# A two-branch token mixer on one core: an eighths fold in the channel transform, and a scan over every second token

## The chip, the cores and the metric

The kernel runs on one core of one Trainium2 chip. The metric is the device time of one execution in microseconds (us), as the median of several runs.

## The reference

The input x has S = 2048 tokens of D = 1024 channels in bf16. Two branches are mixed per token:

```python
g = sigmoid((x * gate_w).sum(-1, keepdims=True))
a = irfft2(rfft2(x) * (w_r + 1j * w_i))           # over tokens and channels
# b: a diagonal state space model
Lam_bar = exp(exp(log_dt) * Lambda)
Bu = einsum("bld,pd->blp", x, B_bar)               # B_bar from B_re, B_im, Lam_bar, Lambda
for t in range(L): h = Lam_bar * h + Bu[:, t]      # complex, 1024 states
b = 2 * einsum("blp,dp->bld", h, C).real + x * Dskip
out = g * a + (1 - g) * b
```

## The kernel before

The kernel is written out by hand for five engines: PE (matmul), DVE (vector), ACT (scalar), POOL and SP (DMA issue). Each step of the computation is a Python generator (`turn`, `fold`, `fd`, `unit_mm`, ...), and a long string `ORDER` holds one letter for each next step of one of them; the order of the letters is the order of the instructions in every engine's queue. The four PSUM buffers are dealt out by the string `SLOTS`. The pieces of the recurrence stand in a list `work`, and each letter `v` issues the next one by the index list `PIECES`. No scheduler changes any of it afterwards. An engine runs its queue in order and waits where an operand or a buffer isn't ready.

The spectral branch begins with the channel transform. `turn` and `turn_out` (PE L919, ACT L929) transpose x into `xQ`. x is treated in 16 row groups j. `fold` on DVE (L943 to L954) makes sums and differences of the two halves of the channels, then of the quarters, into `preT`. For the last four groups of instructions (`MIRROR`, that is eight row groups) PE reverses two blocks of the odd half (`mirror`, L970, into `ps_r`) and `fold_odd` on DVE (L976, L977) adds and subtracts them. `fd` multiplies the result with constant tables on PE, `fd_out` brings it to SBUF as `X1` (L449 on ACT, some on DVE), `s1` starts the token transform. Later stages (`s2`, `times_w`, `is1`, `is2`, `spectral`) go through the frequencies and back.

The state space branch works on eight chunks of 256 tokens. `unit_mm` (L398) makes, for each chunk, four groups of 32 matmuls B x into PSUM (`psu`), and `unit_out` (L408, ACT) copies each to a tile `h` in SBUF. There are three such tiles, so chunk 3's first copy must wait until the products of chunk 0 are done. `recur` makes the recurrence a real scan: it multiplies the states with rotation tables (`cross` L347, `along` L350, `join_re` L353, `join_im` L356), adds the carry of the chunk before (L359), runs the scan over the real and the imaginary part (L363), takes the carry of this chunk (L368, L371) and rotates back (L347, L350, `out_re` L374, `out_im` L378). Chunks 0 and 1 go through this in two halves of four state blocks, the other six whole:

```python
work.extend((lambda: cross(1), lambda: along(0), join_re, join_im))
if c:
    work.append(carry_in)
work.extend((lambda: scan(0, 0, n), lambda: scan(1, 0, n)))
if c + 1 < NCH:
    work.extend((carry_part, carry_sum))
work.extend((lambda: cross(3), lambda: along(2), out_re, out_im))
```

`early_mm` (`c_half`, L713) and, for the last tiles, `own_mm` (`c_part`, L727) multiply h with C for token tiles of 128 tokens, two to a chunk. ACT scales the result (L744), and it is stored or added to the spectral part. The tables of the rotation come from `make_tab`: angles (L279, and on DVE), sine and cosine on ACT (from L1106 on), casts to bf16 (L287, L294, on POOL or ACT by `CAST_ACT`). `radii` (L268) writes the radii that the scan reads on POOL. `turn_vectors` (L1080, L1082) brings the parameters into the layout that all this needs. `load_B` fetches B by transposing DMAs.

Of the kernel before, what the change touches and what calls it, by code (L numbers as in the profile page):

```python
# [25 lines left out]
TC = 256  # L26
NCH = S // TC
# [11 lines left out]
CAST_ACT = (5, 6, 7)  # L39
ANG_ACT = (4, 5, 6, 7)  # L40
CARRY_POOL = ()
# [9 lines left out]
)  # L51
SLOTS = (
    "0123012310231023102310230123012031201312031203101230132031231031201312303312013213021021013010320130",
    "1220123203201320130130120321023120320321021023120312301230231201302303120",
)
MIRROR = (6, 7, 8, 9)
ORDER = (
    "xxxTVUVVVaTfVVrrUGTGG|Tfaaa|UafFffftafftUftxFEfTETUFffU22xSEkSTSTArxAfffUAUFTTEUfffUFbxwxbxbbTUEFbfE",
    "1bT~SSUfuFSFAUUUU2bbtbfAF1AtbbtrFttrbEffE11EbEh11SStbttfttttAg1~HtfufhA~tetFSSFrKHrtu1EAvfAEhtttvttt",
    "SSFtbbvvvAtEttH1Avthtftv1cttwv1tcthccctttvtcch~HFtvftHvvhuHtvfStEettStAHhtAeKrvFctcvvFhEEHKtvwtcSvtS",  # L60
    "hvvKc1vcc1vAAKKvv1c1v1hcvswcsLMvvveHHekMYsssnNHvvhHnsvvvJWWMvs3vsvNvvsssssnvssnvvs4NMvv4Njvhv553vhvv",
    "YvyJJL46H4vv5WWvhh5vvvMM78Jj7HHmn3nHvv8M44m6MnN77WW5jv+Yy5vvv3M845+mNY8nMJJMyvvv+467hvHMh5vN7N34vHmh",
    "4J8m+6n3h8v77HmH+55v4n64JMvNnMYy5vW83n+v7N474vJ568vYmmNJ7dh7NWj+v58v5vyvvd88MhvHHm8+MJm6h+n378vv7Hh8",
    "J+d4Y4YX5vv5NnJH6XXv7ny7mNNm8+hn8hvqivvvvvJvqyHihYivvyiqhivqqiYvNImvni+qJJmHIIiini+HinvdIIH+vvIIIqIN",
    "IiiiNmI+vvIInvvImvyJqii%NJINIJYJYmhvvv+vvvlylzvhHmplpzZZH+mZZZhlZvhPPRR++zyRRRlQDQHzRZZmRHZ+ZRZvoOZD",
    "QvlpDzzPovOvQBvZZlpPYvZZvBZDZRDRRRvzQDoloOBzoQOopZOoPOBlzlZRoDDZZvBZZRpQvzCvYZZvZZBZZPRDoQoo9RQQ9yRR",
    "0RRyCooD099C9Y990DD0D0Y00",
# [6 lines left out]
HALF_PI = float(np.pi / 2)  # L74


def _host_consts():
# [9 lines left out]
    Ge = np.stack([G[0, :H, :, e::2] for e in range(2)])  # L87
    Gf = np.concatenate([G[0, :P, :, 2 * f::4].reshape(P, P) for f in range(2)], axis=1)
    Go = np.stack([G[1, :, :, e::2] for e in range(2)], axis=1)
# [3 lines left out]
    for u in range(4):  # L93
# [25 lines left out]
    angM = 2 * np.pi * (((64 * (f % 32) + 16 * (f // 32) + np.arange(16)[None, :, None]) * np.arange(32)[None, None, :]) % S) / S  # L119
# [11 lines left out]
        G=b16(np.concatenate([Go.reshape(4, P, 4 * K // 4).transpose(1, 0, 2).reshape(P, 4 * K),  # L131
                              Ge.reshape(2, 2, P, H).transpose(2, 0, 1, 3).reshape(P, 4 * H), Gf], axis=1)),
# [10 lines left out]
def kernel(  # L143
# [19 lines left out]
    out2 = out[0]  # L163

    hc = _host_consts()
    cG = nc.inline_tensor(hc["G"], name="c_G").ap()
# [49 lines left out]
    tau_i = tmp.tile([P, TC], I32, name="tau_i")  # L216
    nc.gpsimd.iota(tau_i, pattern=[[1, TC]], base=0, channel_multiplier=0)

# [4 lines left out]
    tab = tabp.tile([P, 4, 8, TC], BF16, name="tab")  # L223
# [6 lines left out]
    fft["G"] = pre.tile([P, 4 * K + 5 * H], BF16, name="G_sb")  # L230
# [19 lines left out]
    def load_G():  # L250
        for a, b in ((4 * K, 4 * K + 5 * H), (0, 2 * K), (2 * K, 4 * K)):
            nc.sync.dma_start(out=fft["G"][:, a:b], in_=cG[:, a:b])
            yield
# [9 lines left out]
    def cast(i):  # L263
        return nc.scalar.copy if i in CAST_ACT else nc.gpsimd.tensor_copy

    def radii():
        for jb in range(8):
            nc.gpsimd.tensor_copy(out=rz[:, jb, :], in_=r_sb[:, jb:jb + 1].to_broadcast([P, TC]))  # L268
            nc.gpsimd.memset(rz[:, jb, 0:1], 0.0)
            yield  # L270

    def make_tab(jp):
        sh = [P, 2, TC]
        js = slice(2 * jp, 2 * jp + 2)
        ang = tmp.tile(sh, FP32, name="ang", tag="ang")
        for j in range(2):
            jb = 2 * jp + j
            if jb in ANG_ACT:
                nc.scalar.activation(out=ang[:, j], in_=tau_f, func=ACT.Copy, scale=thp[:, jb:jb + 1])  # L279
            else:  # L280
                nc.vector.tensor_scalar_mul(out=ang[:, j], in0=tau_f, scalar1=thp[:, jb:jb + 1])
            yield
        sn_f = tmp.tile(sh, FP32, name="sn_f", tag="sn_f")
        cs_f = tmp.tile(sh, FP32, name="cs_f", tag="cs_f")
        yield from sincos(tmp, ang, sh, sn_f, cs_f, "rot")
        yield
        cast(2 * jp)(out=tab[:, 1, js, :], in_=sn_f)  # L287
        yield
        t1 = tmp.tile(sh, FP32, name="t1")
        t2 = tmp.tile(sh, FP32, name="t2")  # L290
        for j in range(2):
            nc.scalar.activation(out=t1[:, j], in_=sn_f[:, j], func=ACT.Copy, scale=ci[:, 2 * jp + j:2 * jp + j + 1])
        yield
        cast(2 * jp + 1)(out=tab[:, 0, js, :], in_=cs_f)  # L294
        yield
        for j in range(2):
            jb = 2 * jp + j
            nc.scalar.activation(out=t2[:, j], in_=cs_f[:, j], func=ACT.Copy, scale=ci[:, jb:jb + 1])
        yield
        for j in range(2):  # L300
            jb = 2 * jp + j
            nc.vector.scalar_tensor_tensor(out=tab[:, 2, jb, :], in0=cs_f[:, j], scalar=cr[:, jb:jb + 1], in1=t1[:, j],
                                           op0=ALU.mult, op1=ALU.subtract)
            yield
        for j in range(2):
            jb = 2 * jp + j
            nc.vector.scalar_tensor_tensor(out=tab[:, 3, jb, :], in0=sn_f[:, j], scalar=cr[:, jb:jb + 1], in1=t2[:, j],
                                           op0=ALU.mult, op1=ALU.add)
            yield

    rz = tabp.tile([P, 8, TC], FP32, name="rz")
    carry = cpool.tile([P, 2, 8], FP32, name="carry")
# [5 lines left out]
    def halloc():  # L318
        pool = hpool[hcount[0] % (NHA + NHB) >= NHA]
        hcount[0] += 1  # L320
        return pool.tile([P, 2, 8, TC], BF16, name="h")
# [7 lines left out]
    def small_ops():  # L329
        return nc.gpsimd if next(smalls_made) in CARRY_POOL else nc.vector  # L330

    smalls_made = itertools.count()

    def recur(c, js, home):
        n = js.stop - js.start
        on_in, on_part, on_sum = (small_ops() for _ in range(3))
        sh = [P, 2, n, TC]
        u = hs[c][:, :, js, :]

        def bc(i):  # L340
            return tab[:, i:i + 1, js, :].to_broadcast(sh)

        tmps = {}

        def cross(i):
            tmps["s"] = home()
# [869 lines left out]
```

## Time and profile before

| | |
|---|---|
| runs | 307.19 us median of 3 (306.89, 307.19, 309.19) |
| the profiled execution's own time | span of 303.6 us from the first to the last instruction, 3.6 us less than the median of the runs |
| granted clock of PE | 0.999 |
| busy PE, DVE, ACT, POOL | 296.4, 289.3, 188.5, 73.3 us |
| DMA | 59.35 MB, 196 GB/s in the mean |
| first product of h with C | at 82.5 us |

Busy times are of one execution, taken by the profiler. The row of a group has the line and the engine, the tiles written and read, the shape, how often it ran, its busy time in all, and the mean of one in ns; what stands behind the last bar is the idle time just before, with the instruction that ended it. A row of the timeline begins with the start and the duration in us.

### The profile page before, as it was taken

Reading aid. Unit: us, or ns where it says so; the run is one execution under the profiler, and the core shown is the slowest. Engines: PE = TensorE matmul, PEld = TensorE weight load, DVE = VectorE, ACT = ScalarE, POOL = GpSimd, SP = SyncE. Lnnn points to the kernel's source line nnn. Section 1 sums busy time; section 2 is a strip of 40 time slices with the busy share of each in tenths; the row PEclk is TensorE's granted clock in tenths of the full one; section 3 lists DMA queues with packets and bytes.
Section 4 is the critical chain, followed back from the end, with each engine's and each line's share of the span. In section 5 each row is a group of like instructions: output and inputs, shape, how many; then the busy total and the mean of one; then the engine's idle time right before and its main releaser. Section 6 shows DMA issues by size and latency. Waiting matters only on the chain. (4 is left out here: it accounts for less than half of the span.)

```text
span 303.6 us, 6402 instructions
## 1 busy us (share of the span) xinstructions
PE 296.4 (98%) x2568; PEld 197.4 (65%) x2592; DVE 289.3 (95%) x340; ACT 188.5 (62%) x255; POOL 73.3 (24%) x99
## 2 busy tenths in 40 slices
PE   8999999999999999999999999999999999999995
PEld 5664677878864685458553866669657986645543
DVE  2999999999999999999999999999899999999995
ACT  4999999896532383667665865529668774343400
POOL 2100420745893001110210220202011253252330
PEclk9999999999999999999999999999999999999999
DMA  6999999989999599895948798687758876978976
GB/s 208 341 201 194 253 193 310 162 142 154 268 214 241 160 259 219 181 250 189 212 96 258 163 223 225 139 294 147 242 174 185 165 88 135 160 132 143 165 153 181
DMA packets 74157, 59.35 MB, mean 196 GB/s; under 512 B 44904, under 2 KB 61680, under 8 KB 74128
## 3 DMA queue, kind: packets, MB, share of 16 engines
q1 hardware_dynamic: 66560, 49.82, 65.8%
q0 software_dynamic: 6912, 8.69, 23.0%
q10 hardware_dynamic: 656, 0.44, 0.5%
q8 instruction: 20, 0.33, 0.4%
q14 instruction: 9, 0.07, 0.1%
HBM read 27.46 MB, written 23.08 MB: 166 GB/s over the span
## 5 line engine op out<-in xcount | busy, mean ns | idle before, releaser
L398 PE MATMUL psu<-xQ,BT 128*128 128x256 bf16 x1024 | 116.5, 273 | 0.2 <-DVE X L449 0.2
L398 PEld LDWEIGHTS <-BT 128*128 128x128 bf16 x1024 | 99.0, 98 | 17.3 <-issue 4.6
L713 PE MATMUL ps_y<-CT,h 128*128 128x512 bf16 x397 | 92.5, 379 | 0.9
L363 DVE TENSOR_TENSOR_SCAN h<-rz,h 128x2048 bf16<-128x2048 f32 (+1 forms) x20 | 70.8, 3561 | 0.0
L713 PEld LDWEIGHTS <-h 128*128 128x128 bf16 x416 | 39.6, 98 | 46.3 <-issue 2.9
L785 POOL DMA_DIRECT2D y_scratch<-su x20 | 17.3, 902 | 135.7 <-ACT su L779 105.4
L408 ACT CAST h<-psu 128x1024 bf16<-128x1024 f32 x32 | 32.3, 1011 | 18.7 <-PE psu L398 13.1
L350 DVE TENSOR_TENSOR h<-h,tab 128x4096 bf16<-128x4096 bf16 (+1 forms) x20 | 37.1, 1859 | 0.1
L744 ACT ACTIVATE ye<-ps_y,omg 128x512 f32<-128x512 f32 x26 | 17.9, 689 | 26.3 <-PE ps_y L713 11.8
L347 DVE TENSOR_TENSOR xQ<-h,tab 128x4096 bf16<-128x4096 bf16 x12 | 27.4, 2284 | 1.0 <-ACT h L408 1.0
L603 ACT CAST X<-ps_s 128x1024 bf16<-128x1024 f32 x16 | 16.2, 1010 | 14.6 <-PE ps_s L594 11.2
L727 PE MATMUL ps_q<-CT,h 128*128 128x512 bf16 (+2 forms) x110 | 21.3, 348 | 0.2
L817 ACT ACTIVATE BT<-ps_id,gB 128x1024 bf16<-128x1024 f32 x14 | 15.3, 1114 | 9.9 <-PE ps_id L810 5.7
L671 ACT CAST ZT<-ps_is 128x1024 bf16<-128x1024 f32 x16 | 15.8, 1017 | 6.2 <-PE ps_is L661 6.2
L637 ACT CAST C<-ps_is 128x1024 bf16<-128x1024 f32 x16 | 15.7, 1011 | 5.1 <-DMA xQ<-in_A_x_dram 3.4
L851 POOL DMA_DIRECT2D BT<-y_scratch x10 | 13.1, 1452 | 19.7 <-DVE BT L846 13.3
L727 PEld LDWEIGHTS <-h 128*128 128x128 bf16 x112 | 10.3, 98 | 10.4 <-DVE h L378 0.5
L779 ACT ACTIVATE su<-xs,omg 128x512 f32<-128x512 bf16 x20 | 14.2, 723 | 4.1 <-DMA y_scratch<-su 2.2
L929 ACT COPY xQ<-pt 128x1024 bf16<-128x1024 bf16 x12 | 12.2, 1082 | 1.3 <-PE pt L919 1.3
L449 ACT CAST X<-ps_fd 128x1024 bf16<-128x1024 f32 x12 | 12.3, 1062 | 1.0 <-PE ps_fd L439 0.9
L617 DVE TENSOR_TENSOR UV<-X,Wb 128x2048 bf16<-128x2048 bf16 x8 | 9.6, 1220 | 0.6 <-ACT ye L744 0.6
L617 DVE TENSOR_TENSOR UV<-X,raw 128x2048 bf16<-128x2048 bf16 x8 | 9.8, 1223 | 0.2 <-ACT X L604 0.2
(200 smaller groups left out, 397.3 us busy)
## 6 DMA issues: line engine op xcount, KB each, us to landing
y_scratch<-ye SPq DMA_DIRECT2D x20, 256.0 KB, 4.6
y_scratch<-su POOLq DMA_DIRECT2D x20, 256.0 KB, 4.7
Bb<-turn_scratch SPq DMA_DIRECT2D x16, 256.0 KB, 5.2
turn_scratch<-C SPq DMA_DIRECT2D x16, 256.0 KB, 4.1
raw<-turn_scratch SPq DMA_DIRECT2D x8, 512.0 KB, 4.3
xs<-in_A_x_dram SPq DMA_DIRECT2D x13, 256.0 KB, 3.9
out_dram<-BT SPq DMA_DIRECT2D x11, 256.0 KB, 4.3
CT<-in_A_x_dram SPq DMA_DIRECT2D x5, 512.0 KB, 6.1
```

Source lines behind the costliest of these rows:

```text
L347: nc.vector.tensor_mul(out=tmps["s"], in0=u[:, ::-1], in1=bc(i))
L350: nc.vector.tensor_mul(out=u, in0=u, in1=bc(i))
L363: nc.vector.tensor_tensor_scan(out=seg, data0=rz[:, js.start + j:js.start + j + m].rearrange("p j t -> p (j t)"), data1=seg, initial=0.0, ...
L398: nc.tensor.matmul(psu[:, j, :], lhsT=BT[4 * q + j][:, ri, d8, :], rhs=xQ[:, c, d8, :], start=(d8 == 0), stop=(d8 == 7))
L408: nc.scalar.copy(out=hs[c][:, ri, 4 * q:4 * q + 4].rearrange("p b (q j) -> p b q j", j=32), in_=psus.pop((c, q, ri)).rearrange("p b (j q) ...
L603: nc.scalar.copy(out=X2, in_=ps2s[g][b])
L617: nc.vector.tensor_mul(out=UV, in0=X2s.pop((g, b)).unsqueeze(1).to_broadcast([P, 2, 2, K]), in1=fft["Wb"][g // 2 % 2][:, :, at:at + 1, :]. ...
L671: nc.scalar.copy(out=ZT[:, 4 * kp:4 * kp + 4, :, 4 * G:4 * G + 4].rearrange("p (c r) n g -> p c r n g", c=2), in_=pszs.pop((G, kp)).rearra ...
L713: nc.tensor.matmul(psy, lhsT=hs[c][:, ri, jb, P * tq:P * (tq + 1)], rhs=CT[ri][:, jb, 512 * dh:512 * (dh + 1)], start=(i == 0), stop=(i == ...
L727: nc.tensor.matmul(psq, lhsT=hs[c][:, ri, jb, P * tq:P * (tq + 1)], rhs=CT[ri][:, jb, at:at + n], start=(i == 0), stop=(i == 15))
L744: nc.scalar.activation(out=ye, in_=psys[tb][:, K * hf:K * (hf + 1)], func=ACT.Copy, scale=omg[:, tb:tb + 1])
L785: nc.gpsimd.dma_start(out=y_dram[tb, hf], in_=xgs[tb, hf], accum_op=ALU.add)
```

## The change

Three things change together, and the order of all instructions is written anew.

The channel transform: all 16 row groups are folded down to eighths of the channels on DVE, the mirroring on PE is gone, and `fd` multiplies with smaller tables. There are two groups of a single row group and seven of two.

The scan: h keeps even and odd tokens apart, in rows of 128 tokens with two elements of padding in front (`SEG` = 130). The even tokens, multiplied with the radius beforehand through the tables, are added to the odd ones (`both`); the scan runs over the odd tokens alone with the squared radius, real and imaginary parts of four state blocks in one instruction; the carry is written into the padding. ACT then multiplies the odd states, shifted by one, with the squared radius (`shift`, four instructions for each scan), and DVE adds that to the even tokens (`add_shift`). The tables get scaled copies for even tokens, on POOL, and two more exponentials.

Token tiles hold the even or the odd tokens of a chunk instead of 128 neighbouring ones, so x and out are read and written by rows that are two tokens apart.

```diff
-CAST_ACT = (5, 6, 7)
+CAST_ACT = ()
+PAIRED = [(j, 1) for j in range(2)] + [(j, 2) for j in range(2, 16, 2)]
...
-    out2 = out[0]
+    x_t, out_t = (t[0].rearrange("(c s a) d -> c a s d", s=HC, a=2) for t in (A_x, out))
...
 def make_tab(jp):
...
+        wave = tmp.tile([P, 2, 2, 2, HC], FP32, name="wave", tag="wave")
+        even = wave[:, :, 0]
+        yield from sincos(tmp, ang, sh, wave[:, 1], wave[:, 0], "rot")
+            nc.gpsimd.tensor_scalar_mul(out=even[:, :, j], in0=even[:, :, j], scalar1=r_sb[:, jb:jb + 1])
+        yield
+        (nc.scalar.copy if jp in CAST_ACT else nc.gpsimd.tensor_copy)(out=tab[:, 0:2, q, :, js, :], in_=wave)
+            nc.gpsimd.tensor_scalar_mul(out=even[:, :, j], in0=even[:, :, j], scalar1=ir2[:, jb:jb + 1])
+        yield
+        turned = tmp.tile([P, 2, 2, 2, HC], FP32, name="turned")
...
 def recur(c, qs, home):
...
+        def both():
+            nc.vector.tensor_add(out=odd, in0=odd, in1=even)
         def carry_in():
...
+            for q in range(n):
+                pads = seg[:, q, 1, :, :, 0:PAD]
+                if c:
+                    a, b = (ck[:, :, i, 4 * (qs.start + q):4 * (qs.start + q) + 4].rearrange("p r j -> p j r").unsqueeze(3).to_broadcast([P, 4, 2, PAD])
+                            for i in range(2))
+                    nc.vector.tensor_add(out=pads, in0=a, in1=b)
+                else:
+                    nc.vector.memset(pads, 0.0)
+        def scan(q):
+            at = seg[:, q, 1].rearrange("p j r t -> p (j r t)")
+            nc.vector.tensor_tensor_scan(out=at, data0=rz[:, qs.start + q].rearrange("p j r t -> p (j r t)"),
+                                         data1=at, initial=0.0, op0=ALU.mult, op1=ALU.add)
         def carry_part():
...
+            for q in range(n):
+                at = slice(4 * (qs.start + q), 4 * (qs.start + q) + 4)
+                nc.vector.tensor_mul(out=ck[:, :, :, at], in0=seg[:, q, 1, :, :, SEG - 1].rearrange("p j r -> p r j").unsqueeze(1).to_broadcast([P, 2, 2, 4]), in1=rot[:, :, :, at])
+        def shift(q):
+            if q == 0:
+                tmps["z"] = home().rearrange("p (q j r) t -> p q j r t", q=2 * n, j=4)
+            for j in range(4):
+                jb = 4 * (qs.start + q) + j
+                nc.scalar.activation(out=tmps["z"][:, q, j], in_=seg[:, q, 1, j, :, PAD - 1:SEG - 1], func=ACT.Copy, scale=r2[:, jb:jb + 1])
+        def add_shift(q):
+            nc.vector.tensor_add(out=even[:, q], in0=even[:, q], in1=tmps["z"][:, q].rearrange("p j r t -> p (j r) t"))
         def out_re():
...
+            nc.vector.tensor_add(out=u[:, :, 0], in0=u[:, :, 0], in1=tmps["s"][:, :, 0])
+            done[c] = done.get(c, 0) + 4 * n
         def out_im():
...
+            nc.vector.tensor_sub(out=u[:, :, 1], in0=u[:, :, 1], in1=tmps["s"][:, :, 1])
+            done[c] = done.get(c, 0) + 4 * n
+        work.extend((lambda: cross(1), lambda: along(0), join_re, join_im, carry_in, both))
+        for q in range(n):
+            work.append(lambda q=q: scan(q))
+            shifts.append(lambda q=q: shift(q))
         if c + 1 < NCH:
...
+            work.append(carry_part)
+        for q in range(n):
+            work.append(lambda q=q: add_shift(q))
         work.extend((lambda: cross(3), lambda: along(2), out_re, out_im))
+    def shift_out():
+        for k in range(2 * NCH):
+            shifts[k]()
...
 def fd():
...
+            psd = psf[j] = psum([P, 2, 4, P], "ps_fd")
+            for f in range(2):
+                nc.tensor.matmul(psd[:, 0, 2 * f], lhsT=preTs[j][:, 5 - f, :], rhs=G_sb[:, f], start=True, stop=True)
+            for part in range(2):
+                nc.tensor.matmul(psd[:, 0, 1::2], lhsT=preTs[j][:, 6 + part, :], rhs=G_sb[:, 2 + 2 * part:4 + 2 * part],
+                                 start=(part == 0), stop=(part == 1))
+            for odd in range(2):
+                for part in range(2):
+                    at = 6 + 4 * odd + 2 * part
+                    nc.tensor.matmul(psd[:, 1, 2:0:-1] if odd else psd[:, 1, 0::3], lhsT=preTs[j][:, 2 * odd + part, :],
+                                     rhs=G_sb[:, at:at + 2], start=(part == 0), stop=(part == 1))
...
 def fold():
...
+        for j, n in PAIRED:
             if j % 2 == 0:
...
+                pairs["t"] = gta.tile([P, 2, 8, P], BF16, name="preT", bufs=2)
+                pairs["s"] = gta.tile([P, 2, 8, P], BF16, name="sums", bufs=1)
             at = slice(j % 2, j % 2 + n)
             for i in range(n):
                 preTs[j + i] = pairs["t"][:, (j + i) % 2]
+            t, s = pairs["t"][:, at], pairs["s"][:, at]
             lo, hi = (x_gjq[:, :, d:d + 4, :, j:j + n, :].rearrange("p c d g j q -> p d g c j q") for d in (0, 4))
             apart = lambda t: t.rearrange("p j d (g c q) -> p d g c j q", g=2, c=NCH)
...
+            nc.vector.tensor_add(out=apart(s[:, :, 4:8]), in0=lo, in1=hi)
+            yield
+            nc.vector.tensor_sub(out=apart(s[:, :, 0:4]), in0=lo, in1=hi)
+            yield
+            nc.vector.tensor_sub(out=t[:, :, 6:8], in0=s[:, :, 4:6], in1=s[:, :, 6:8])
+            nc.vector.tensor_add(out=s[:, :, 4:8:2], in0=s[:, :, 4:6], in1=s[:, :, 6:8])
+            nc.vector.tensor_sub(out=t[:, :, 0:5:4], in0=s[:, :, 1:5:3], in1=s[:, :, 3:7:3])
+            nc.vector.tensor_add(out=t[:, :, 1:6:4], in0=s[:, :, 1:5:3], in1=s[:, :, 3:7:3])
+            yield
+            nc.vector.tensor_scalar_mul(out=t[:, :, 0:2], in0=t[:, :, 0:2], scalar1=SQRT_HALF)
+            nc.vector.tensor_sub(out=t[:, :, 2:4], in0=s[:, :, 0:4:2], in1=t[:, :, 0:2])
+            nc.vector.tensor_add(out=t[:, :, 0:2], in0=s[:, :, 0:4:2], in1=t[:, :, 0:2])
...
-        nc.scalar.activation(out=r_sb, in_=are, func=ACT.Exp)
+        for r, k in ((r_sb, 1.0), (r2, 2.0), (ir2, -2.0)):
+            nc.scalar.activation(out=r, in_=are, func=ACT.Exp, scale=k)
```

The lines that go are those of the functions shown above, and of `mirror` and `fold_odd`. `PIECES`, `SLOTS` and `ORDER` are replaced as a whole. In the new order the parameter vectors are turned ahead of x, all transposing loads of B come behind both loads of turned x, and 13 groups of `unit_mm` stand ahead of the first product with C, where 11 stood.

More of the change, by code (lines that the diff above doesn't have):

```diff
@@ L472, in s1_out @@
             else:
[L473 removed]
+                if j < 15:
+                    last = tmp.tile([P, 2 if j == 14 else 1, 2, K], BF16, name="A1_last", tag=("ang", "rot_kk", "wave")[j - 12])
+                A1 = last[:, j // 15]
             (nc.vector.tensor_copy if j in S1_DVE else nc.scalar.copy)(out=A1, in_=pss.pop(j))
```

257 lines of the change are left out of this document (91 added, 166 removed), and 12 rows, old and new, of the table PIECES.

## The prediction

> **What bounds the kernel now.** I read the busy shares first, then the busy time in stretches of 10 us, then the places where DVE hands work to PE, and last the groups of instructions by shape.
>
> ```profile
> PE 296.4 (98%) x2568; PEld 197.4 (65%) x2592; DVE 289.3 (95%) x340; ACT 188.5 (62%) x255; POOL 73.3 (24%) x99
> ...
> 0.00:10.00 10.00, 8.59 (x76) 5.86 (x78) 4.13 (x20) 5.54 (x11) 2.98 (x17) 1.00 0.77 256
> 10.00:20.00 10.00, 9.36 (x90) 6.12 (x91) 9.58 (x29) 10.00 (x12) 0.56 (x2) 1.00 1.16 273
> 170.00:180.00 10.00, 9.95 (x109) 7.72 (x108) 10.00 (x9) 8.28 (x13) 1.74 (x2) 1.00 0.93 220
> 240.00:250.00 10.00, 10.00 (x102) 9.04 (x101) 9.43 (x19) 8.29 (x9) 4.55 (x5) 1.00 0.74 108
> ...
> 81.40 0.68 DVE L374 TENSOR_TENSOR h<-h,su 128x1024 bf16<-128x1024 bf16 x1
> ...
> L713 PE MATMUL ps_y<-CT,h x397: 376/379/390, 82.5 to 276.1; 128*128 128x512 bf16 x199
> ```
>
> The stretches give, after their length, the busy time of PE, weight loads, DVE, ACT and POOL, then the clock (full everywhere), the DMA share and GB/s. PE and DVE are both full from about 10 us on, so neither alone is the bound: the order of the work keeps them in step. Only in the first 10 us is there room (PE 8.59, DVE 4.13). The last two rows are the tightest hand-over. DVE finishes the last real-part sum of the scan's chunk 0 at 81.40 + 0.68 = 82.1 us, and PE begins the first product of the scan with C at 82.5. What makes DVE late at this point stops PE, and what PE loses nobody gives back, since it is at 98%. The three h buffers forbid going round it: chunk 3's eviction needs the buffer that only chunk 0's y products free.
>
> **The change: PE.**
>
> ```profile
> L398 PE MATMUL psu<-xQ,BT 128*128 128x256 bf16 x1024 | 116.5, 273 | 0.2 <-DVE X L449 0.2
> L713 PE MATMUL ps_y<-CT,h 128*128 128x512 bf16 x397 | 92.5, 379 | 0.9
> ...
> 100.84 3.66 PE L398 MATMUL psu<-xQ,BT 128*128 128x256 bf16 x32
> ```
>
> A matmul's busy time goes by its columns: 116.5 us / (1024 x 256) = 0.444 ns for one. The channel transform of one row group takes 3072 columns unmirrored and 1792 mirrored, plus four mirroring matmuls of 512: 8 x 3072 + 8 x 1792 + 4 x 512 = 40,960. After the change each of the 16 takes 2 x 128 + 2 x 256 + 4 x 256 = 1792, together 28,672. The 12,288 columns saved are worth 12,288 x 0.444 = **5.5 us**, all of it ahead of 82 us. If nothing else bound, the end would come at 303.6 - 5.5 = 298.1 us.
>
> In the new order 13 unit groups (32 matmuls of L398 each) stand ahead of the first y product instead of 11. That moves two groups of 3.66 us forward and adds nothing to the sum. The y products of one half take 8 x 92.5 / 397 = 1.9 us before they need the second half of chunk 0. So PE will want DVE's last output of chunk 0 at 82.5 - 5.5 + 7.3 + 1.9 = **86.2 us**.
>
> **The change: DVE in all.**
>
> ```profile
> L363 DVE TENSOR_TENSOR_SCAN h<-rz,h 128x2048 bf16<-128x2048 f32 x12 | 52.7, 4416 | 0.0
> L363 DVE TENSOR_TENSOR_SCAN h<-rz,h 128x1024 bf16<-128x1024 f32 x8 | 18.1, 2278 | 0.0
> L353 DVE TENSOR_TENSOR h<-h,xQ 128x2048 bf16<-128x2048 bf16 x6 | 7.3, 1222 | 0.0
> L353 DVE TENSOR_TENSOR h<-h,su 128x1024 bf16<-128x1024 bf16 x4 | 2.7, 679 | 0.0
> L350 DVE TENSOR_TENSOR h<-h,tab 128x4096 bf16<-128x4096 bf16 (+1 forms) x20 | 37.1, 1859 | 0.1
> ```
>
> The scan costs 52.7 + 18.1 = 70.8 us now. Over odd tokens it is 16 scans of 1040 elements, at 2.278 / 1024 x 1040 = 2.31 us, or 37.0: 33.8 less. It isn't free. Before it the even tokens are added to the odd ones (4 sums of 1024 at 0.68 and 6 of 2048 at 1.22, 10.0 us); after it the shifted states go onto the even ones (16 sums of 1024 at 0.68, 10.9 us). The products keep their elements, and the wider rows (128 of 130) are taken at no cost, with rival D for the other case. The small carry instructions are about 4 more, 1 us by the shortest row below. So the scan part is -33.8 + 10.0 + 10.9 + 1 = -11.9 us.
>
> ```profile
> L943 DVE TENSOR_TENSOR preT<-xQ 128x1024 bf16<-128x1024 bf16 (+1 forms) x10 | 6.2, 620 | 0.5 <-ACT xQ L929 0.2 <-PE pt L919 0.2
> L945 DVE TENSOR_TENSOR sums<-xQ 128x1024 bf16<-128x1024 bf16 (+1 forms) x10 | 6.2, 619 | 0.0
> L948 DVE TENSOR_TENSOR preT<-sums 128x512 bf16<-128x512 bf16 (+1 forms) x10 | 3.7, 367 | 0.1
> L950 DVE TENSOR_TENSOR preT<-sums 128x256 bf16<-128x256 bf16 (+1 forms) x6 | 2.2, 369 | 0.0
> L952 DVE TENSOR_TENSOR sums<-sums 128x512 bf16<-128x512 bf16 x4 | 1.7, 425 | 0.1
> L953 DVE TENSOR_TENSOR preT<-sums 128x256 bf16<-128x256 bf16 x4 | 1.4, 344 | 0.1
> L954 DVE TENSOR_TENSOR preT<-sums 128x256 bf16<-128x256 bf16 x4 | 1.1, 283 | 0.0
> L976 DVE TENSOR_TENSOR preT<-preT,ps_r 128x512 bf16<-128x512 bf16 x4 | 2.7, 682 | 0.6 <-PE ps_r L970 0.6
> L977 DVE TENSOR_TENSOR preT<-preT,ps_r 128x512 bf16<-128x512 bf16 x4 | 2.7, 687 | 0.1
> ...
> L945 DVE TENSOR_TENSOR sums<-xQ 128x1024 bf16<-128x1024 bf16 x6 | 4.5, 755 | 0.0
> L943 DVE TENSOR_TENSOR preT<-xQ 128x512 bf16<-128x512 bf16 x4 | 1.7, 430 | 0.1
> ...
> 18.36 0.42 DVE L948 TENSOR_TENSOR preT<-sums 128x512 bf16<-128x512 bf16 x1
> 18.70 0.46 DVE L950 TENSOR_TENSOR preT<-sums 128x512 bf16<-128x512 bf16 x1
> ...
> L1106 DVE TENSOR_SCALAR rot_kk<-ang 128x512 f32<-128x512 f32 x4 | 1.7, 418 | 0.0
> L548 DVE TENSOR_SCALAR Bcol<-Bcol 32x64 bf16<-32x64 bf16 x1 | 0.2, 238 | 0.0
> ```
>
> Folding takes the first nine rows now, 27.9 us. After the change there are seven pairs and two single row groups, each of nine instructions. A pair is 2 x 0.755 + 6 x 0.42 and one scaling by the root of a half. No row has that scaling in bf16; it lies between 0.24 (64 elements, L548) and 0.42 (512 elements of f32, L1106), and I take 0.30. That makes 4.33, and a single one 2 x 0.43 + 6 x 0.29 + 0.27 = 2.87, where 0.29 is the 256-element subtraction shown further down. 7 x 4.33 + 2 x 2.87 = 36.0, so **8.1 us more**. DVE as a whole goes from 289.3 by -11.9 + 8.1 = -3.8 us.
>
> **Where DVE's share falls.** The sum over the kernel hides what decides. All of the 8.1 us lies ahead of chunk 0's end, and most of the scan's gain behind it. Going through both programs' DVE streams up to chunk 0's last sum: 3 scans at 2.31 where there were 4 at 2.28 (-2.2), 3 even-to-odd sums (+2.0), 2 sums of shifted states (+1.4). The start and POOL's part are left.
>
> ```profile
> 4.17 1.06 PE L919 MATMUL pt<-ident,CT 128*128 128x128 bf16 x8
> ...
> DVE vecF L1082 <- PE vps L1080: 4.9, 1, 4.9
> ...
> 8.14 0.29 DVE L948 TENSOR_TENSOR preT<-sums 128x256 bf16<-128x256 bf16 x1
> 8.26 0.42 POOL L268 COPY rz<-r_sb 128x256 f32<-128x256 f32 x1
> 8.34 0.49 DVE L950 TENSOR_TENSOR preT<-sums 128x256 bf16<-128x256 bf16 x1
> ...
> L268 POOL COPY rz<-r_sb 128x256 f32<-128x256 f32 x8 | 4.5, 559 | 0.3 <-ACT r_sb L1091 0.3
> L287 POOL CAST tab<-sn_f 128x512 bf16<-128x512 f32 x3 | 2.4, 805 | 24.0 <-ACT sn_f L1111 24.0
> L294 POOL CAST tab<-cs_f 128x512 bf16<-128x512 f32 x2 | 1.2, 614 | 0.9 <-ACT cs_f L1113 0.9
> ```
>
> DVE now waits 4.9 us for the turned vectors, behind a transpose of x of 1.06. The new order turns the vectors first: a gain between 0 and 1.06, taken as 0.5. POOL gets 16 scalings of 256 elements and 4 casts of 1024 for the 5 casts of 512 that it has now, 15 instructions more. What one costs DVE shows at 8.34: the same subtraction as at 8.14 takes 0.49 beside a POOL copy and 0.29 without, 0.20 more. All 15 would be 3.0 us, none is 0, and with some of them beside DVE's waits I take 10, or 2.0.
>
> [...]
>
> So DVE finishes chunk 0 at 82.1 + 8.1 - 2.2 + 2.0 + 1.4 - 0.5 + 2.0 = **92.9 us**, and PE stands for 92.9 - 86.2 = **6.7 us**. Behind the waiting matmul is all the rest of PE's queue, and behind that ACT's evictions. After 92.9 DVE has 3.8 + 9.3 = 13.1 us less to do than before, so it should not be late a second time, and PE sets the pace.
>
> **ACT and the queues.**
>
> ```profile
> L279 ACT ACTIVATE ang<-tau_f,ang 128x256 f32<-128x256 f32 x4 | 2.0, 510 | 0.0
> ...
> ACT h L408 <- PE psu L398: 13.1, 11, 2.6
> ```
>
> The shift is 64 ACT instructions of 128x256, 64 x 0.51 = 32.6 us, four between each scan and the sum that needs it. ACT has 303.6 - 188.5 = 115 us free, and waits 13.1 of them for PE's unit groups; I take the shift as hidden there. Uncovered it is rival C. The second table of scalings and exponentials costs ACT early, when it is full (10.00 of 10 in the second stretch); its lag ends at the same hand-over, so it isn't added. On SP the 16 transposing loads of B now come behind both loads of turned x, and token tiles are fetched as rows of every second token, with the same 2 KB a row. Both are taken at nothing: the fold and the channel transform on PE cover the loads, and stores start earlier only if PE does.
>
> **Sum.** 303.6 - 5.5 + 6.7 = 304.8 us of span. The median of the runs, 307.19, lies 3.6 over the profiled span, so the time is **308.4**. Its own range: without contention and with the whole 1.06 at the start the stall is 4.1; with 3.0 of it, 0.42 for each scaling (+1.1), no gain at the start, and 1.3 for ACT's fuller start it is 10.6: 305.8 to 312.3.
>
> **The rivals.** *A, faster: the early DVE queue is hardly late.* Independent DVE instructions overlap: at 18.36 + 0.42 the first ends, at 18.70 the second has started, 0.08 earlier. The new fold sets more independent ones in a row; 25 such overlaps are 2.0 us. With no contention (2.0) and 0.24 for a scaling (0.5) DVE is done at 88.4, the stall is 2.2, the end 300.3, the time **303.9**; with no stall 301.7. For it: DVE's idle in the first 10 us (5.9) could absorb some of the fold. Against it: from 10 to 20 us it is at 9.58 of 10, and the fold instructions of one group mostly depend on each other.
>
> *B, slower: POOL and DVE exclude each other.* POOL's extra work is 16 x 0.559 + 4 x 1.23 (twice the 512-element cast of 0.614) - 2.4 - 1.2 = 10.2 us; all of it taken from DVE instead of 2.0 gives 101.1, a stall of 14.9 and **316.6**. It decides once over half of the extra POOL time is added to DVE ahead of 90 us. Against it: 0.20 of 0.42 in the rows above.
>
> *C, slower: the shifts block ACT's queue in the middle.* ACT runs in order; a shift that waits for its scan holds up the evictions behind it, and so PE's PSUM slots. ACT is at 8.28 and 8.29 of 10 in the later stretches, and four shifts add 2.0 each time. If each of the 12 shift groups of chunks 2 to 7 costs PE a quarter of its 2.0 us, it is 6.0 more: **314.4**. It decides once PE shows several waits for evictions of more than 0.5 us after 95 us. Against it: ACT's 13.1 us of waiting for PE now.
>
> *D, the change doesn't do what it says:* with rows of 130 elements the products lose their rate. Twice L350's 37.1 us alone would be some 345.
>
> **How the numbers follow.** About 1% (3 us) can be told from no change here. The forecast gets 0.45 (0.29 within 1% of before, that is up to 310.3, and 0.16 above), A 0.30 (0.24 under 304.1, the rest within), B 0.08, C 0.15, D 0.02. Faster 0.24, same 0.35, slower 0.41. The range reaches down to A without a stall, 301.7, and up to 316, short of B and D.
>
> **What would show it.** Right: PE busy down by 5 to 6 us; the scan group at 16 x 2.3; the fold near 36 us; DVE's last sum of chunk 0 near 93 us, and one PE wait of 4 to 10 us for it at about 86. Wrong: no such wait (A), the DVE fold instructions at 0.6 beside POOL (B), PE waits for ACT spread over the middle (C), products at twice their time (D). A scan much above 2.31, or PE waits at other places than this hand-over, would break the forecast itself.

## The result and the profile after

The changed kernel takes 317.02 us (median of four runs, 316.65 to 317.71) beside 307.04 us for the kernel before. The ratio is 1.032, with a 95% interval from 1.027 to 1.038. In the runs below the kernel before took 305.2 to 305.8 us in the median, and it ran beside each of them, so the comparisons go by ratios. The changed kernel itself was not run again beside them, so differences from it of 1% are not certain.

The page of the changed kernel, then its stretches of 10 us, with the columns as before:

```profile
PE 298.0 (94%) x2588; PEld 197.9 (63%) x2588; DVE 291.8 (92%) x392; ACT 213.5 (68%) x312; POOL 89.0 (28%) x114
...
0.00:10.00 10.00, 8.44 (x78) 5.72 (x79) 4.74 (x19) 5.29 (x9) 1.41 (x9) 1.00 0.79 276
10.00:20.00 10.00, 6.09 (x65) 5.48 (x64) 8.46 (x32) 9.98 (x16) 2.32 (x10) 0.83 1.08 245
20.00:30.00 10.00, 7.25 (x53) 4.25 (x52) 8.91 (x16) 9.97 (x12) 3.73 (x4) 0.85 1.05 187
170.00:180.00 10.00, 10.00 (x113) 6.53 (x112) 9.96 (x11) 8.07 (x14) 0.86 (x1) 1.00 0.89 207
240.00:250.00 10.00, 10.00 (x102) 8.66 (x101) 9.90 (x11) 9.54 (x16) 1.75 (x2) 1.00 0.69 191
```

The loss lies ahead of 100 us. From 10 to 30 us PE is busy 6.09 and 7.25 where it had 9.36 and 9.45, and its granted clock falls to 0.83 and 0.85. In the middle (170, 240) PE is full. PE does not even show the saving in its busy time (298.0 beside 296.4). In part this is because matmuls took longer while the granted clock was 0.50 (the four of L460 1.06 us at 29.40, and 0.60 at 21.61 with a clock of 1.00); in part the profile of the kernel before lacks some matmuls (397 products of h with C are recorded, 416 after).

The hand-over of chunk 0, from the timeline of the changed kernel:

```profile
78.82 0.85 DVE L399 TENSOR_TENSOR h<-h,su 128x1024 bf16<-128x1024 bf16 x1
99.72 0.73 DVE L399 TENSOR_TENSOR h<-h,su 128x1024 bf16<-128x1024 bf16 x1
...
98.13 2.12 PE L734 MATMUL ps_y<-CT,h 128*128 128x512 bf16 x9
100.52 11.83 PE L734 MATMUL ps_y<-CT,h 128*128 128x512 bf16 x54 [0.27 <-DVE h L399]
```

DVE ends chunk 0 at 99.72 + 0.73 = 100.45 us. PE begins its first product at 98.13 (82.5 before), and waits only 0.27 us for the second half. Both engines are 14 us later than PE's own work gives (82.5 - 5.5 + 7.3 = 84.3), and they arrive together. The forecast wait of 6.7 us at this place isn't there; PE had lost the time earlier. Up to its first product it is busy for 86.3 of 98.1 us, so it stands for 11.9 us, where it stood for 2.8 before (79.7 busy of 82.5). The other 4.8 us are busy time over the 81.5 that its work should take (79.7 - 5.5 + 7.3). Some 2.8 of them are an estimate for the half clock: PE was busy for 6.5 us of the two stretches at 0.50 (13.3 to 16.7 and 26.9 to 30.4 us), and 6.5 x (1 - 0.60 / 1.06) = 2.8 by the times of L460. PE's longest waits (who waited, for whom, us in total, how often, the longest):

```profile
PE pt L940 <- ACT xQ L950: 3.9, 2, 3.6
PE ps_s L480 <- ACT xQ L950: 1.3, 1, 1.3
PE ps_fd L460 <- DVE preT L976: 1.3, 2, 0.7
```

All its waits for ACT come to 8.6 of the 11.9 us. The longest of them, with ACT's queue beside it and then stretches of 2 us:

```profile
9.85 0.61 ACT L1111 ACTIVATE rot_kk<-ang 128x512 f32<-128x512 f32 x1
10.37 0.61 ACT L1112 ACTIVATE wave<-ang 128x512 f32<-128x512 f32 x1
10.99 1.28 ACT L1092 ACT_TABLE_LOAD   x1
12.28 0.41 ACT L1092 ACTIVATE r_sb<-are 128x8 f32<-128x8 f32 x3
12.59 2.82 ACT L950 COPY xQ<-pt 128x1024 bf16<-128x1024 bf16 x3
...
13.63 3.45 PE L940 MATMUL pt<-ident,CT 128*128 128x128 bf16 x32 [3.60 <-ACT xQ L950]
...
10.00:12.00 2.00, 0.03 (x1) 0.00 (x0) 1.40 (x7) 2.00 (x3) 0.00 (x0) 1.00 1.02 409
12.00:14.00 2.00, 0.37 (x4) 0.36 (x4) 1.48 (x10) 1.99 (x6) 1.03 (x6) 0.82 1.18 232
14.00:16.00 2.00, 2.00 (x21) 1.87 (x19) 1.86 (x7) 2.00 (x5) 1.29 (x6) 0.50 0.84 176
16.00:18.00 2.00, 2.00 (x25) 1.92 (x23) 1.86 (x5) 2.00 (x3) 0.00 (x0) 0.82 1.18 265
```

ACT makes the sine of the first table, loads a function table and takes the exponentials while turned blocks of x wait in PSUM. (The exponentials stand between two sines, which costs two loads of 1.28 us, at 10.99 and 24.00.) PE needs their buffers and stands for 3.60 us; its granted clock is 0.50 from 13.3 to 16.7 us.

### The profile page after: what moved, and what is told of

Read it like the earlier page. It is cut to its first block, busy times and chain, and to the rows that moved or that the text cites. A ratio compares the mean times of both kernels' runs of the same rounds, so it can differ in the third digit from the quotient of the medians.

```text
span 315.9 us, 6542 instructions
## 1 busy us (share of the span) xinstructions
PE 298.0 (94%) x2588; PEld 197.9 (63%) x2588; DVE 291.8 (92%) x392; ACT 213.5 (68%) x312; POOL 89.0 (28%) x114
## 5 line engine op out<-in xcount | busy, mean ns | idle before, releaser
L806 POOL DMA_DIRECT2D y_scratch<-su x20 | 18.5, 1011 | 129.3 <-ACT su L800 113.9
L436 ACT CAST h<-psu 128x1024 bf16<-128x1024 f32 x32 | 31.6, 1012 | 15.3 <-PE psu L426 10.4
L353 DVE TENSOR_TENSOR h<-h,tab 128x4096 bf16<-128x4096 bf16 (+1 forms) x20 | 37.4, 1868 | 0.5
L376 DVE TENSOR_TENSOR_SCAN h<-rz,h 128x1040 bf16<-128x1040 f32 x16 | 36.9, 2319 | 0.2
L350 DVE TENSOR_TENSOR xQ<-h,tab 128x4096 bf16<-128x4096 bf16 x12 | 27.4, 2282 | 1.6 <-ACT h L436 1.5
L389 ACT ACTIVATE xQ<-h,r_sb 128x256 bf16<-128x256 bf16 x48 | 20.3, 502 | 3.0 <-DVE h L376 2.9
L748 PEld LDWEIGHTS <-h 128*128 128x128 bf16 x112 | 10.2, 98 | 12.0 <-DVE h L399 1.0
L298 POOL TENSOR_SCALAR wave<-wave,r_sb 128x256 f32<-128x256 f32 x8 | 8.2, 1030 | 31.0 <-ACT wave L1114 31.0
L940 PE MATMUL pt<-ident,CT 128*128 128x128 bf16 x96 | 8.6, 256 | 4.3 <-ACT xQ L950 3.9
```

The source lines that it names most:

```text
L350: nc.vector.tensor_mul(out=tmps["s"], in0=u[:, :, ::-1], in1=bc(i))
L353: nc.vector.tensor_mul(out=u, in0=u, in1=bc(i))
L376: nc.vector.tensor_tensor_scan(out=at, data0=rz[:, qs.start + q].rearrange("p j r t -> p (j r t)"), data1=at, initial=0.0, op0=ALU.mult, o ...
L389: nc.scalar.activation(out=tmps["z"][:, q, j], in_=seg[:, q, 1, j, :, PAD - 1:SEG - 1], func=ACT.Copy, scale=r2[:, jb:jb + 1])
L436: nc.scalar.copy(out=hs[c][:, q, :, :, ri, PAD:].rearrange("p a b (q t) -> p b a q t", q=8), in_=psus.pop((c, q, ri)).rearrange("p b (t a ...
L748: nc.tensor.matmul(psq, lhsT=hs[c][:, jb // 4, tq, jb % 4, ri, PAD:], rhs=CT[ri][:, jb, at:at + n], start=(i == 0), stop=(i == 15))
```

## Experiments

**Is it ACT's early queue, or POOL's scalings, or both?** The first run moves letters of the order (V and a are steps of the small vectors, t of the tables, U evicts turned x); the second leaves the scalings out; the third does both; the fourth, later and on another chip, keeps POOL's work and takes away only those who wait for it.

```diff
 e1: VVVVV aatt .. aa2xtVaaUUU .. FfftTbUUrfb  ->  VVVVVV aatt .. 2xUUU .. FffaattTbUUaarfb
 e2, e3 (left out), e8 (turned aside):
-  nc.gpsimd.tensor_scalar_mul(out=even[:, :, j], in0=even[:, :, j], scalar1=r_sb[...])   # and ir2
+  nc.gpsimd.tensor_scalar_mul(out=aside, in0=even[:, :, j], scalar1=r_sb[...])           # e8
```

> The changed kernel with four steps moved on ACT: the three exponentials of the radii stand right behind the first exponential (no two extra table loads), and the sine and cosine of the small vectors and of the first table stand behind the first evictions of the turned x. Theory P (PE's time lost ahead of 32 us, idle 3.6 us for xQ and at half clock behind it, is lost for good): 317.0 falls to 308 to 311 us. Theory D (DVE's chunk 0 ends at 100.4 us whatever PE does): at most 3 us less, 314 or more, and PE now waits 5 us or more ahead of the second half of its first product with C.

> The changed kernel without the 16 scalings of the table on POOL (left out, so the even tokens' tables are not scaled). Theory P: DVE is done with chunk 0 some 4 to 6 us earlier, but PE comes to its first product at 98 us as before: 316 to 317.5 us. Theory D, with POOL and DVE in each other's way: 311 to 313 us.

> Both edits together (scalings left out, ACT's early steps moved). If PE's early loss and DVE's chunk 0 end at the same point by chance, neither edit alone gives much and both together give 8 to 11 us: 306 to 309 us. By theory P alone the same as the first run, by theory D alone the same as the second.

> The changed kernel with the 16 scalings of the table still done on POOL, but into a tile that nothing reads (so the even tokens' tables are not scaled, and nobody waits for a scaling). If POOL and DVE are in each other's way, as slow as the changed kernel, a ratio of 1.032; if the chain from sine over POOL's scalings and ACT to DVE's tables costs the time, as fast as without the scalings, 1.025.

The ratios to the kernel before were 1.033 (1.029 to 1.036) for the first, 1.025 (1.023 to 1.027) for the second, 1.021 (1.017 to 1.024) for the third and 1.034 (1.029 to 1.039) for the scalings turned aside. The row of PE's timeline where the second half of chunk 0 arrives, in this order:

```profile
98.56 12.04 PE L734 MATMUL ps_y<-CT,h 128*128 128x512 bf16 x55 [0.27 <-DVE h L399]
...
95.97 12.04 PE L734 MATMUL ps_y<-CT,h 128*128 128x512 bf16 x55 [0.18 <-DVE h L399]
...
94.39 12.04 PE L734 MATMUL ps_y<-CT,h 128*128 128x512 bf16 x55 [0.27 <-DVE h L399]
...
98.85 12.04 PE L735 MATMUL ps_y<-CT,h 128*128 128x512 bf16 x55 [0.27 <-DVE h L400]
```

ACT's order is worth 2 us at the hand-over and nothing that the ratios can tell. Neither of the two theories of the first run holds as a whole: its 315.2 us fit the second, but PE waited 0.27 us instead of 5. The second run's 312.8 us are what the second theory expects. With ACT's steps moved PE waits for DVE's fold instead (3.4 and 1.8 us for `preT`, where it had waited 1.6). The third run was expected at 306 to 309 us and took 312.1.

The scalings are worth 100.52 - 95.97 = 4.5 us at the hand-over. Of these, 1.7 come from the chain over POOL and ACT to DVE's tables (98.85; DVE's waits of 1.8 us for `turned` are gone there) and 2.9 from POOL being busy at all. Each of these numbers is of one execution. How POOL and DVE meet, in the changed kernel:

```profile
58.40 2.46 POOL L298 TENSOR_SCALAR wave<-wave,r_sb 128x256 f32<-128x256 f32 x2 [7.16 <-ACT wave L1114]
58.95 0.85 DVE L362 TENSOR_TENSOR h<-h 128x1024 bf16<-128x1024 bf16 x1
59.72 0.43 DVE L969 TENSOR_TENSOR preT<-sums 128x512 bf16<-128x512 bf16 x1
60.19 0.50 DVE L970 TENSOR_TENSOR sums<-sums 128x512 bf16<-128x512 bf16 x1
...
42.07 1.31 POOL L300 CAST tab<-wave 128x1024 bf16<-128x1024 f32 x1
42.52 1.14 DVE L971 TENSOR_TENSOR preT<-sums 128x512 bf16<-128x512 bf16 x1
...
60.93 1.11 POOL L300 CAST tab<-wave 128x1024 bf16<-128x1024 f32 x1
61.07 1.25 DVE L972 TENSOR_TENSOR preT<-sums 128x512 bf16<-128x512 bf16 x1
```

Beside the two scalings DVE's instructions take 0.85, 0.43 and 0.50 us, where they take 0.68, 0.42 and 0.42 alone: 0.17 us more at most, and next to nothing for the one in the middle. Ahead of chunk 0's end 22 DVE instructions began during a scaling, and none grew by more than 0.20 us (1.5 us in all). Beside a cast it is another matter. Two DVE instructions of 0.42 us that began during a POOL cast took 1.14 and 1.25 us and ended 0.28 us after the cast did (43.66 beside 43.38, 62.32 beside 62.04). The row at 8.34 in the kernel before, beside a POOL copy of 0.42 us, looks like the casts': DVE's instruction ended 0.15 us after the copy (8.83 beside 8.68). The casts are in all four runs, so the 2.9 us belong to the scalings; the 1.5 us are the part of it that the rows show directly.

**Which part of the change costs?** The fold alone in the kernel before, then only for row groups 8 to 15, where it takes the place of the mirroring (the edit in words):

```diff
-            if not mirrored(j): ... else: ...          # fold(), fd(): old forms
+            seven more instructions and 1792 columns   # as in the changed kernel; second run: j >= 8 only
```

> The kernel before with the fold by eighths alone: old scan, old order, four single row groups and six pairs. By the prediction's steps PE has 5.5 us less and DVE at least 8 us more ahead of chunk 0's end: PE comes to its first product at 77 us, DVE at 90, a stall of 13 us, some 315 us. If DVE has slack there, 302 us.

> The kernel before with the fold by eighths for row groups 8 to 15 alone, in place of the mirroring: same DVE work within 1.5 us (a mirrored pair is 4.34 us by its rows, a pair by eighths 4.3 to 4.7), four mirroring matmuls and 8 x 0.17 us of channel transform less on PE, 2.3 us. Where DVE has to do no more, the fold pays: 303 to 305 us beside 305.4. If the eighths themselves cost (their small instructions one behind the other), 307 or more.

The fold alone gave 1.036 (1.035 to 1.038), 316.5 us; for the late groups alone 1.003 (1.001 to 1.005), 306.6 us. So in the old order it is the early fold that costs nearly 10 us (by the difference of the two), and the late one gains nothing either. The first product began at 93.39 in the one and 83.66 in the other; the last two rows are PE's longest waits ahead of it in the first run:

```profile
93.39 3.63 PE L709 MATMUL ps_y<-CT,h 128*128 128x512 bf16 x16
...
83.66 3.63 PE L737 MATMUL ps_y<-CT,h 128*128 128x512 bf16 x16
...
PE ps_s L458 <- DVE X L445: 6.7, 3, 3.1
PE ps_fd L438 <- DVE preT L950: 2.3, 3, 1.3
```

The time of the first run is what was expected (some 315 us), but not for the expected reason. There is no stall of 13 us at the first product: from 76 us on PE runs into it without a wait. It lost the time ahead of 40 us, where it is busy for 28.6 us (37.2 before), waiting for folded rows and for evictions that stand behind the fold in DVE's queue, and at a lower clock (0.83 granted in the mean from 10 to 40 us). The agreement of the number is luck.

Then the scan in the old order: the whole change, the scan with the fold of late groups, and that without POOL's scalings. A shift (`^`) stands right behind its scan; the order in words:

```diff
-v(scan re) v(scan im) v(carry_part) v(carry_sum) v(cross)
+v(carry_in, chunk 0) v(both) v(scan) ^ v(carry_part) v(add_shift) v(cross)
```

> The whole change (fold by eighths for all groups, scan over odd tokens, even and odd token tiles) in the order of the kernel before: same letters, each scan followed by its shift on ACT, the even-to-odd sum ahead of the scan, the sum of shifted states ahead of the rotation back. If the new order is what makes the change slow (PE idle at 10 us behind ACT's table steps), this is faster than the changed kernel: 310 us or less. If the parts do it, it is as slow as the fold alone plus what the scan costs ahead of chunk 0: 316 to 321.

> The scan over odd tokens (with its tables and token tiles) in the order of the kernel before, with the fold of the run that cost 1.4 us (eighths for groups 8 to 15 alone, 306.6 us). By the prediction's terms DVE has 2.3 x 3 - 4 x 2.28 + 2 x 0.7 + 2 x 0.7 = 0.6 us more ahead of chunk 0's end, and POOL's scalings cost 2 to 4.5: 309 to 312 us. If the odd scan pays for itself, since DVE has 13 us less to do behind, 304 to 306.

> The same without the 16 scalings of the table on POOL (left out, the even tokens' tables are not scaled). If POOL in DVE's way is the scan part's cost, 3 to 4 us less than the run with them.

The ratios were 1.211 (1.204 to 1.219), 1.175 (1.173 to 1.178) and 1.149 (1.143 to 1.154). The expectations of the first two missed this by 50 us, and the scalings cost 11 us here instead of 3 to 4. The waits of the second (waiting, waited for, us in total, times, longest) show why:

```profile
ACT xQ L381 <- DVE h L368: 25.3, 8, 10.1
DVE xQ L342 <- ACT h L428: 15.7, 3, 6.4
DVE tab L306 <- ACT turned L301: 14.6, 7, 7.8
ACT turned L301 <- POOL wave L296: 12.1, 6, 5.1
```

ACT stands for a scan with evictions queued behind the shift, and DVE stands for those evictions. This is rival C's mechanism. How much of the 55 us over the same fold in the kernel before (362.2 beside 306.6) is due to it is not shown: the scalings cost 11 of them, and no run takes the shifts away. The new order avoids it: there ACT waited for scans 3.6 and 2.9 us. So the scan needs a new order, though the one that it got loses the front.

**Early fold or late fold, in the new order?** The seven small instructions of a fold group are left out for some row groups, and the first two write `preT` directly (the transform of these groups is then not the reference's); everything else is in place. An earlier run in which the early groups are folded in the old way, and one of that with ACT's order of the first experiment, stand beside it.

```diff
+            if j < 8:        # e12; e13: j >= 8; e14 and e15: always; e15 also with the edits of e3
+                nc.vector.tensor_add(out=apart(t[:, :, 4:8]), in0=lo, in1=hi)
+                yield
+                nc.vector.tensor_sub(out=apart(t[:, :, 0:4]), in0=lo, in1=hi)
...
+                continue
```

> The changed kernel with the fold by eighths for row groups 8 to 15 alone; groups 0 to 7 are folded to quarters of the even half and halves of the odd half, as before, with their larger tables on PE. DVE has 2 x 1.5 + 3 x 2.3 = 9.9 us less ahead of chunk 0's end, PE 8 x 0.59 = 4.7 us more. If DVE's fold sets chunk 0's end, that comes at 90 to 92 us instead of 100.4 and the ratio to the kernel before falls from 1.032 to about 1.005 (307 us beside 305.4). If the fold on DVE is hidden, PE's 4.7 us make it 1.047.

> The first of these runs (eighths for groups 8 to 15 alone in the changed kernel) with ACT's early steps moved as well, the exponentials together and the first table's sine behind the evictions. If DVE and ACT both held back chunk 0, another 2 us less than the first: a ratio of about 1.00 to the kernel before.

> The changed kernel with most of the early fold left out: row groups 0 to 7 get the first sum and difference only, the seven instructions after them are gone (so these groups' transform is not the reference's), PE's work and the loads stay. DVE has 3 x 3.26 + 2 x 2.08 = 13.9 us less before about 40 us. If DVE's fold sets the front, chunk 0 ends 10 us or more earlier and the time is 306 or less (ratio 1.00). If ACT's queue sets it (full from 10 to 30 us), at most 2 us less.

> The same for row groups 8 to 15: DVE has 4 x 3.26 = 13 us less between 40 and 75 us. If DVE alone sets chunk 0's end from 40 us on, 10 us or more are won (305); if PE is as late, only the 3.6 us that PE waits from 40 to 90 us (311 to 312).

> Both: DVE has 27 us less ahead of chunk 0's end. What is left of the time over the kernel before is then not DVE's fold. If fold is the whole cause: 300 us or less. If ACT and PE in the first 40 us are as late by themselves: 309 or more.

> All three causes out at once: the small fold instructions left out, POOL's scalings left out, ACT's early steps moved. If these three hold the front, PE comes to its first product near the 84 us that its own work gives (82.5 - 5.5 + 7.3) and the time is 298 to 302 us.

The old fold for early groups gave 1.035 (1.030 to 1.041), and 1.038 (1.035 to 1.042) with ACT's order; both missed what was expected of them (about 1.00, or 1.047 for the first). These two also load 0.8 MB more of tables ahead of x, so PE waits 2.8 and 3.1 us for x, and they don't separate the causes cleanly. Leaving out the early fold gave 1.035 (1.032 to 1.038), the late one 1.018 (1.014 to 1.022), both 1.021 (1.017 to 1.024), all three causes 1.013 (1.009 to 1.016). Their first products:

```profile
97.97 2.12 PE L734 MATMUL ps_y<-CT,h 128*128 128x512 bf16 x9
...
93.30 13.99 PE L734 MATMUL ps_y<-CT,h 128*128 128x512 bf16 x64
...
93.81 13.99 PE L734 MATMUL ps_y<-CT,h 128*128 128x512 bf16 x64
...
91.81 13.99 PE L734 MATMUL ps_y<-CT,h 128*128 128x512 bf16 x64
```

Taking 13.9 us of early fold from DVE changes nothing: DVE then just idles, ACT and PE are as late, and chunk 0 ends at 100.30 us (100.45 with the whole fold). Taking 13 us of late fold wins 4.8 us at the first product, and PE then takes all 64 products in one row. But PE is still 9 us behind the 84.3 of its own work, even with the whole fold gone. With all three causes out it is 7.5 us behind, and the run missed its expectation (298 to 302 us) by 8. Its trace shows where: from 30 us to the first product at 91.81 PE is busy without a gap, so all of the 7.5 us lie ahead of 30: PE stands there for 4.9 us more than before, and the other 2.6 are put down to the lower clock, as an estimate (0.68 granted from 20 to 30 us). It waits for the eviction that now stands behind the moved sine, and for the loads of x, 3.5 us at the longest:

```profile
PE ps_s L480 <- ACT xQ L950: 3.5, 1, 3.5
PE pt L940 <- DMA CT<-in_A_x_dram: 1.8, 3, 1.1
```

**What holds PE then?** With the fold left out, ACT's queue is made shorter: four of the twelve evictions of x go to DVE, the exponentials stand together, and the first sines behind the last eviction of x. The second run does that with the fold complete, and the third moves the sines one step further back.

```diff
-            nc.scalar.copy(out=x_gjq[:, :, :, :, j, :]...
+            (nc.vector.tensor_copy if j in (4, 6, 8, 10) else nc.scalar.copy)(out=x_gjq[:, :, :, :, j, :]...
 order: e16, e17: .. FUUU aattaa EEEtS;   e18: .. FUUU EEE aattaa tS
```

> The changed kernel with the small fold instructions left out for all row groups, so that DVE is idle in places ahead of 40 us, and ACT's early queue made shorter with that room: four of the twelve evictions of the turned x (row groups 4, 6, 8, 10) go to DVE, the exponentials stand together, and the steps of the small vectors and of the first table's sine stand behind the last eviction of x. With the fold left out alone PE began its first product at 93.8 us. If ACT's queue is what holds PE in the first 30 us, PE begins at 85 to 89 us now and the time is 303 to 308 us; if it is something else (the loads of x, PE's own order), 311 us as without it.

> The same shorter ACT queue in the changed kernel with its fold complete. DVE, which has the long fold, gets 4 evictions of about 1.1 us more. If DVE's fold is the second cause at the same hand-over, nothing is won: 315 to 319 us; if ACT alone is the cause, 307 to 310.

> As the run with the fold left out and ACT's early queue shortened (313.3 us), but the steps of the small vectors and of the first table's sine stand one place later, behind the next evictions of the channel transform, so that no DVE instruction in front of those waits for ACT's sine. There PE had gained 6.6 us by 20 us and lost 7.1 again in that one wait. If ACT's queue is what delays PE's first product, PE keeps most of the gain: first product at 86 to 90 us, 304 to 308 us. If the gain is lost again at another place, 310 us or more, and the front has no single holder.

The ratios were 1.025 (1.021 to 1.029), 1.068 (1.064 to 1.073) and 1.025 (1.021 to 1.029). All three missed the gain that ACT's queue as the only cause would give, and the second was slower than either of its two cases: with the fold complete the four evictions come late on DVE, and PE waits 5.1 us for them. In the first run PE is 6.6 us ahead of the run with the fold left out at 20 us and loses 7.1 again; in the third it is 6.3 us ahead and loses 6.6. The waits of the first and, behind the dots, of the third:

```profile
PE ps_s L480 <- DVE X L467: 7.1, 1, 7.1
DVE lb L1144 <- ACT SC L1122: 7.7, 1, 7.7
...
PE zps_g L1008 <- DVE CT L494: 6.6, 1, 6.6
DVE lb L1144 <- ACT SC L1122: 5.2, 1, 5.2
```

So ACT's queue does hold PE in the first 20 us. That relieving it makes the first product earlier is not shown: each time the gain was lost behind a DVE instruction that waits for the postponed sine, and PE's granted clock was low around it (0.70 and 0.79 in the two stretches of 10 us from 20 to 40 us in the first run, 0.77 and 0.89 in the third). A version with neither wait wasn't run, so it stays open whether any order of this front keeps the gain. The even and odd token tiles were not tested alone. No version was faster than the kernel before.

## Why the prediction was wrong

The direction of its sum was right (a loss ahead of chunk 0's hand-over that eats the saving on PE), the size was not: 308.4 with a range to 316, measured 317.02. Its place was also wrong. In spans the miss is 315.9 - 304.8 = 11.1 us, 7.6 of it up to the hand-over (100.5 instead of 92.9) and 3.5 behind it.

- *PE's saving.* The 5.5 us of columns are there as work (a row group of `fd` starts 0.77 us after the last, where plain ones took 1.3). They never reached the end.
- *PE wants chunk 0's second half at 86.2 us: the step that failed.* It came at 98.13 + 2.1 = 100.2. The step moved PE's own work and left its waits as they were; the sum lets PE and DVE meet at chunk 0's hand-over alone. But PE needs evictions from ACT and DVE all through the front, and the new order puts ACT's sine and exponentials ahead of some of them (3.60 us, and a granted clock of 0.50 from 13.3 to 16.7 us). PE stood for 11.9 us instead of 2.8, and was busy for 4.8 us longer than its work. With the three causes out together PE's first product still came at 91.8, with none of them out at 98.1. The prediction had ACT's full early queue in its rows (10.00 of 10) and put it aside as "its lag ends at the same hand-over"; in its upper bound it counted 1.3 us.
- *DVE is done at 92.9 us.* It was 100.45. Up to there DVE's busy time grew by 14.9 us (74.4 to 89.3), where the sum has 11.3, and its waiting by 3.5 (7.7 to 11.2), where the sum has 0.5 less. In the work, the nine fold rows sum to 38.6 us, not 36.0; some of this is POOL in the way (37.7 without the scalings), so it can't be added to the 2.9 of contention, which was taken as 2.0. In the waits are 1.8 us for the chain of sine, POOL, ACT and DVE tables, 1.0 for the exponentials and 0.8 for PE, all at nothing in the sum. Nor does DVE's work alone set this end: with 13.9 us less of it ahead of 40 us chunk 0 ended at 100.30. Scans at 2.32 us, and sums at 0.67 to 0.74 where POOL was not in the way, came as priced:

```profile
L971 DVE TENSOR_TENSOR preT<-sums 128x512 bf16<-128x512 bf16 x7 | 3.8, 539 | 0.2
L972 DVE TENSOR_TENSOR preT<-sums 128x512 bf16<-128x512 bf16 x7 | 4.0, 565 | 0.0
L974 DVE TENSOR_SCALAR preT<-preT 128x512 bf16<-128x512 bf16 x7 | 2.7, 391 | 0.2
L376 DVE TENSOR_TENSOR_SCAN h<-rz,h 128x1040 bf16<-128x1040 f32 x3 | 6.9, 2322 | 0.0
```

- *Where DVE's share falls.* The fold alone in the old order gave the time that this step gives (316.5 us for some 315), but by luck: PE lost it ahead of 40 us, waiting for DVE's evictions, and not in one stall at the first product. In the new order only the late half of the fold counts, since in front of 40 us ACT and PE are as late as DVE.
- *Behind the hand-over.* 211.9 us were forecast from there to the end (304.8 - 92.9); it took 315.9 - 100.5 = 215.4. With the late fold left out it is 309.3 - 95.4 = 213.9, though PE waits only once more, for 0.7 us; so 2.0 us are missing from the sum and stay unexplained. The changed kernel waits for the last chunk besides:

```profile
296.58 0.39 PE L748 MATMUL ps_q<-CT,h 128*128 128x512 bf16 x1 [0.53 <-DVE h L395]
297.72 13.81 PE L748 MATMUL ps_q<-CT,h 128*128 128x512 bf16 x79 [0.74 <-DVE h L399]
```

- *The 3.6 us at the end of the sum.* They are the median of the runs less the span of one profiled execution. In an execution of its own the difference is 1.8 (317.71 beside a span of 315.9; later runs of the kernel before took 305.38 at a span of 303.6). The rest was the difference between two executions, so on like terms the forecast is 306.6, further off than it looks.
- *The rivals.* A (DVE hardly late) is out. B came nearest in its number (316.6), by luck: two DVE instructions took 0.72 and 0.83 us longer beside a POOL cast, but the scalings, most of POOL's extra work, cost an instruction that began during one 0.20 us at most, and 2.9 us were lost in all, not 10.2. C's mechanism is real in the old order and next to nothing in the new one. D is out: the products keep their rate (37.4 us for the 20 of L353, 37.1 for the 20 of L350 before).

## What to carry to other kernels

Where two engines are in step with no slack, a saving on one is worth nothing until the step that both meet at comes earlier; ask of each engine in turn, ACT included, when it would get there. When work is reordered, carry the waits along with the work: an early eviction that moves behind a table load stops the engine that needs its buffer (PE for 3.60 us here). A stretch that is late for several reasons at once may show little gain when one of them is removed, so remove them together as well before judging any.

## What was not expected of the hardware

PE stood for 3.60 us ahead of 13.63, and its granted clock was 0.50 from 13.3 to 16.7 us: 32 transposes took 3.45 us, where 16 had taken 1.06 at full clock, so the wait of 3.6 us cost some 5 by estimate (3.60 + 3.45 - 2 x 1.06 = 4.9). The second stretch at half clock, from 26.9 to 30.4 us, shows more: no such wait stood ahead of it. From 23.5 to 26.9 us PE was busy for 1.32 of 3.40 us, and it had not waited longer than 1.31 us at a time. From 47.4 to 50.8 us it was busy for 2.39 of 3.40, and its clock was 1.00 there and behind it. So here half clock followed a string of short waits as it followed the long one. How much waiting it takes was not shown.

Two DVE instructions that began during a POOL cast ended 0.28 us behind it (1.14 and 1.25 us instead of 0.42). A DVE cast that began during one at 28.04 took 1.23 us, and 1.22 elsewhere. Of the 22 that began during POOL's scalings none lost more than 0.20 us.
